# A fused attention and mixing kernel: wide key copies from one key buffer, and a newly searched order of all operations

## Chip, cores and metric

The kernel runs on one core of a Trainium2 chip. The metric is the time of one execution in microseconds (us) on the device. Several runs give a median, and one more execution was recorded by the hardware profiler. The core has TensorE (PE, matmuls), VectorE (DVE), ScalarE (ACT), GpSimd (POOL), and SyncE (SP), which here only issues transfers (DMA) between the device's memory and the on-chip memory.

## What is computed

Four batches of 768 positions, eight heads of 64, model width 512. Attention is over a local window and over 24 block summaries; what follows is a complex gate, a mixing over positions and a channel layer.

```python
def _attn_ref(q, k, v):                    # B, H, S, D = 4, 8, 768, 64
    block, window = (32, 16)
    k_sum = k.reshape(B, H, nb, block, D).max(axis=3)
    v_sum = v.reshape(B, H, nb, block, D).mean(axis=3)
    scores_l = scale * np.matmul(q, k.transpose(0, 1, 3, 2))
    mask_l = np.abs(pos[:, None] - pos[None, :]) < window
    scores_s = scale * np.einsum('bhsd,bhnd->bhsn', q, k_sum) + np.log(block)
    scores_all = np.concatenate([np.where(mask_l, scores_l, -1e9), scores_s], axis=-1)
    a = softmax(scores_all)
    return np.matmul(a, np.concatenate([v, v_sum], axis=2))
...
    theta = x @ w_theta
    zr, zi = x * np.cos(theta), x * np.sin(theta)
    y = np.einsum('ts,bsd->btd', w_tok_r, zr) + np.einsum('ts,bsd->btd', w_tok_i, zi)
    u = x + y
    return u + np.maximum(u @ w_ch, 0.0)
```

## The kernel before

**Tiles.** A tile is 128 positions of one batch, so there are 6 per batch and 24 in all; "tile n" counts through all batches. Heads are kept in four pairs, one pair filling the 128 partitions. For each tile the kernel does, on PE unless named otherwise:

- scores (L464): queries against a buffer `k` that holds, for each pair and each half of the tile, the 24 summaries and 94 neighbouring keys. `k` is filled by copies on ACT or POOL (L457): once a batch one copy of the summaries `ks` (192 elements a partition), and for each tile four copies of 2 pairs x 94 = 188 elements, one for each half of the tile and half of the pairs.
- softmax: DVE multiplies by the mask and takes sums (L502), ACT takes the exponential (L506);
- turns (L515, L519): transposes on PE, copied out by ACT or DVE;
- products with the values (L489) against two buffers `v`. Each half's values come by a DMA into one of four buffers; 24 rows of it hold the value summaries `vs`, which are copied there for the first tiles of a batch (L438). Norming is at L527 to L536;
- the second turn (L545), after which ACT copies out `x` (L296), or splits it into a high and a low part;
- theta (L570 for the first six tiles, as raw float32; L575 after that, split into parts);
- the gate: POOL or DVE reduces the angle (L587), DVE (L588) and ACT (L584, L593, L599) make sine and cosine, and DVE multiplies (L610), giving `zh`, and `zl` as the low part;
- a mixing step (L638) for each tile, half of the channels and pair of matrices, added into PSUM banks `m0`, `m1`, `m2`. At the end of a batch DVE adds the banks to `x` (L657).

**Keys and summaries.** At the start of a batch (`prepass`, L378 to L419) the keys come by DMA into two buffers `kn` of two pairs each; DVE takes the maxima of blocks (L387) and the sums of values `vt` (L409; for the first batch PE does it, L393).

**Weights.** These come as 64-bit floats and are turned into float32 by integer operations: a magnitude (L348 on ACT, L350 on DVE), a clamp (L352, POOL or DVE), a shift and two combinations on DVE (L354, L356, L359). This runs for all matrices in the first 85 us. High and low parts are made at L296/L298 and L305.

**The out stage** works on the last `u` with a Strassen-like scheme: operands are prepared (L679, L305), 56 products run on PE (L754), and DVE and ACT add them (L761, L766, L773).

**What sets the order.** All operations of the kernel (about 2000) are recorded once, and `schedule` (L226) replays them in the order of a table of numbers, `ORDER` (from L55), in which each number is a record and a letter behind it picks ACT (a), DVE (d) or POOL (g). Each engine takes its operations in the order in which the table has them, and SP issues the transfers likewise, waiting until the buffer of each is free. So a transfer whose buffer is still read holds up all transfers behind it.

Of the kernel before, what the change touches and what calls it, by code (L numbers as in the profile page):

```python
# [19 lines left out]
P = 128  # L20
NT = S // P
# [34 lines left out]
6 8 7 9 10 12 11 13 27g 22 29a 28a 31a 30a 32 1 33 41 42 46 34 14 0 161g 162g 66 16 4 44 45 37 35 67d 43 47 38 48 39 36 68d  # L56
40 69 70 3 71 18 15 17 19 163g 164a 60 2 51 691g 23 156 25 20 21g 49 24a 50a 165 61d 62g 63 64 26g 72 206 157 78 159 160g
158g 211g 209g 210g 212a 52d 166 5 167 168 169 53 174 176 177 175 213 170 171 73a 84 85 262 208 207 86 87 57a 54a 173 178
172 180 181 179 55 58 56d 59d 182 184 183a 185a 74g 75 65 193 79d 80g 186 214 217 216 81 76 82 222 215 77 83 266a 194a 220
187a 224 225 188 223 189d 268a 95a 267a 226 218 221 190a 191 96g 228 219 229 265a 227 97 192d 98 195 196 197 198 199 230 232  # L60
269 100a 200d 201 241 101g 231a 233a 270 272 273 322a 242a 202a 318 263 234 320 264 389 88 319 89 90 91 92 93 271 102 94 99
105 103 235a 236 278 280 281 274 106a 238a 239 323a 277 279 324g 107g 237d 240d 321a 275 284 276 285 282 283 108 104 109 243
244 245 246 247 248d 111d 286 288 325 287a 289a 203 249 112g 290 326 328 329 113 110 204 114 205 115 297 298a 299 254 300
250a 116a 251 291a 394a 121a 393a 255 301 256 302 253 334 336 327 292 335 332 333 338 339 293a 340 392a 330 331 303 117g
122d 252 118 123 119 124 120 125 304d 294a 126a 131a 337 295 305 310 342 311 257 296a 695a 341 353 344 395a 343a 345a 354a
306a 396 127g 132d 128 133 129 134 130 135 346 136a 141a 397 398 405 406 408 412 409 410 350a 307 355 356 357 358 137g 142d
138 143 139 144 140 308 145 347a 146a 359 151a 147d 360d 148 312 313 366 368 367 152g 348 361 351 349a 352a 693a 362a 424
425a 363 149 153 150 154 155 369 374 391 446 390 448 376 378 380 364 375 309 379 399 407 381 445 504 382 384 426 427 428 429
430 258a 689a 260a 431g 694g 696g 432 433a 434 400 377 401 411 402 450a 453a 404 454g 452g 451g 403 435 439 437 440 438 496
415 383 385 386 365 455 387 413 414d 416a 456 459 463 458 457 462 314g 315g 560 509a 692d 388g 449g 511g 460 510a 461 512a  # L70
259g 447g 498 417 497 464 467 465 418d 466 421a 422 513 468 470 469 471 505 507 508a 419 420d 423d 483 474 472 473d 484a
475a 514 517 516 261g 690d 506d 316d 485 486 476 487 488 564a 563a 370g 515 522 524 523 565a 518 566a 480a 525 557d 567 526
520 477a 527 519 521 489 529 528 481 478 479d 482d 530 532 531a 533a 490d 491 492d 493 697 499 698d 700d 699 534 568 570 436
494 574 541d 569 576 577 578 535a 536 538d 582 571 542d 573 575 572 605a 606a 537d 579 583 539 540d 701 702 543 545 703 317g
604g 580 595a 596d 495 584 704 581 586 705 706g 585d 707 546 551 636a 372a 544 770 587a 708a 607a 771a 637g 371g 601 608
654a 561 642a 547 553 549 562 588 589a 649 648 724 603 735 602 373g 609 653g 652g 441g 443a 444g 442g 500g 502g 501g 503g
773d 610 772 643g 613 611 612 614 617 619 621 592d 590 651a 593 618 591d 594d 620 616 622 615 623 624 597 774 598 775 625
599 776 627 777 709 778 626a 628d 555a 556d 779d 780 781a 638 600 639 640 644 655 629 799 641 645 646 685 647 686 687 802a
630a 656 633d 558g 559d 634 631 710 725 683d 664 800a 782 739g 659 663 738a 657 661 741a 666 684d 711 712d 801 713d 667 658
# [12 lines left out]
1068g 1009 996d 1034 1038 1003 1005 1182 1041 1183 1018 1134 1136 1019 1065 1064 1004 1043 1013 1184 1014 1185 1116a 1117
1058a 1042d 1007 1044d 1186 1187g 1118 1188 1189d 1015 1071 1045 1207 1016 1054 1056 1072 1046d 1190 1080 1081 1055 1057
1099a 1085 1148a 1075 1079 1146a 1191 1120a 1135 1049d 1053g 1059d 1100d 1121d 1208d 1050 1147g 1149g 1060 1062 1061 1063
1101 1103 1128 1143 1130 1228 1066 1138 1145 1144 1083 1119 1047 1048d 1073 1082 1074 1078 1087 1076 1086 1051d 1209 1077
1210a 1084 1211 1088 1212 1104 1213 1090 1214 1102 1150 1089a 1091a 1215 1092 1129 1137 1192 1216d 1217 1122d 1266 1126 1124
1127 1125 1151 1159 1161 1162 1218a 1267d 1093a 1153 1139 1268 1163 1193a 1160 1157 1096a 1166 1269a 1165 1152 1097 1094
1154 1095d 1155 1158 1156 1098a 1164 1270 1140 1271 1141 1169 1272 1167 1273 1142d 1006 1229 1131 1233a 1123g 1236g 1237g
1235a 1219 1230g 1197 1195 1198 1196 1194g 1220 1222d 1234a 1238 1308 1370 1231 1008 1168d 1170a 1274 1275g 1276 1171 1205
1201 1199 1172a 1316a 1223d 1239 1242 1241 1203 1277d 1287 1290a 1288a 1175a 1278 1309 1204 1010 1310g 1311 1247 1248 1289  # L100
1279 1250 1240 1173 1249 1176 1221 1174d 1177d 1315g 1243 1252 1251 1245 1246 1254 1314g 1232g 1253 1244 1313a 1224 1225
1291 1226 1292 1283 1293 1255 1294 1257 1227 1317 1256a 1295 1258a 1259 1280 1296d 1297 1345 1318 1319 1263a 1323 1264 1326
1320 1329 1321 1346d 1348a 1322 1298a 1333 1281d 1206 1421 1200 1372 1202 1371 1328 1260d 1261 1347 1373g 1374g 1330 1324
# [132 lines left out]
def c_dve(n, kind="psum"):  # L236

    return {"psum": 0.065 + n * 1.045e-3, "two": 0.05 + n * 1.045e-3, "fast": 0.045 + n * 0.52e-3}[kind]
# [30 lines left out]
def attn_moe(tc, qg, vg, kT, vT, vn, wth, wtr, wti, wch, cst, out, tune=TUNE):  # L269
# [154 lines left out]
    def att_tile(b, i, due):  # L424
# [19 lines left out]
        else:  # L444
# [512 lines left out]
```

## Time and profile before

| | us |
|---|---|
| median of 3 runs | 459.95 |
| the runs | 459.4, 459.95, 460.04 |
| the profiled execution | 458.47 |
| its span | 456.7 |
| granted TensorE clock | 1.00 |

The span is what the profiler's trace covers; the 1.8 us around it belong to the execution too. The profile's groups have one row for a line, engine, operation and tile: count, busy time and mean time in ns, then the idle time of the engine just before them with what ended it. A timeline row has the start, the length, the engine, the line and the operation, with its outputs and inputs, and in brackets the idle time before it and its releaser. In names, `k<-kn` reads: written `k`, read `kn`.

### The profile page before, as it was taken

The numbers are of one execution on the slowest core, as the hardware profiler recorded it, in microseconds if no ns is written. First come the engines' busy times: TensorE is split into PE (matmuls) and PEld (weight loads), VectorE is DVE, ScalarE is ACT, GpSimd is POOL, SyncE is SP. The second block draws the span as 40 slices with busy tenths as digits, with TensorE's granted clock in tenths as the row PEclk, the third lists the DMA queues.
The fourth block names the chain that finished last, engine by engine and source line by source line (L and its number), as shares of the span: only waits on it lengthen the run. The fifth ranks groups of instructions, "written<-read, shape, count | busy, mean of one in ns | idle before, by whom it ended". The sixth has DMA issues, their size and how long they took to land.

```text
span 456.7 us, 9383 instructions
## 1 busy us (share of the span) xinstructions
PE 436.5 (96%) x3552; PEld 355.6 (78%) x3552; DVE 336.3 (74%) x926; ACT 270.8 (59%) x608; POOL 103.0 (23%) x126
## 2 busy tenths in 40 slices
PE   1998999999999999999999999999999999999997
PEld 1465555667888788888888888888878878899996
DVE  3799899698296755776667644765455789999997
ACT  2699996888676677756376585676334316323420
POOL 0421103626910021211031102011111300163340
PEclk9999999999999999999999999999999999999999
DMA  8999965220458222310723400310004710000077
GB/s 286 336 329 282 414 201 155 89 60 4 132 177 275 83 71 72 105 54 12 252 79 105 132 4 1 117 37 1 0 1 140 253 70 0 1 0 1 18 267 269
DMA packets 25005, 55.80 MB, mean 122 GB/s; under 512 B 2944, under 2 KB 8320, under 8 KB 24960
## 3 DMA queue, kind: packets, MB, share of 16 engines
q1 hardware_dynamic: 24960, 55.20, 37.1%
q8 instruction: 28, 0.46, 0.4%
q14 instruction: 17, 0.14, 0.1%
HBM read 45.75 MB, written 9.44 MB: 121 GB/s over the span
## 4 chain that ended last, share of the span: by engine, by line
PE 58%; DVE 12%; issue 1%; ACT 0%; DVEq 0%
PE m L638 31%; PE t L575 9%; PE m L754 4%; PE c L754 4%; PE pa L489 3%; DVE wt L305 3%; PE s L464 3%; PE pa L515 2%; DVE cb L679 2%; PE t L545 2%; DVE x L657 1%; DVE cu L773 1%; PE t L754 1%; DVE zl L305 1%; DVE wth L305 1%
## 5 line engine op out<-in xcount | busy, mean ns | idle before, releaser
L638 PE MATMUL m<-wt,zh 128*128 128x512 f32 (+1 forms) x768 | 181.1, 359 | 2.8 <-DVE zh L610 1.5
L638 PEld LDWEIGHTS m<-wt,zh 128*128 128x128 f32 x768 | 122.5, 188 | 35.1 <-issue 14.3
L638 PE MATMUL m<-wt,zl 128*128 128x512 f32 x336 | 85.9, 336 | 0.0
L506 ACT ACTIVATE e<-e,st 128x118 f32<-128x118 f32 x192 | 64.0, 388 | 22.7 <-DVE st L502 21.9
L638 PEld LDWEIGHTS m<-wt,zl 128*128 128x128 f32 x336 | 51.2, 188 | 7.3
L502 DVE CUSTOM_DVE_ANT_0 e<-s,cs 128x118 f32<-128x118 f32 x192 | 45.3, 273 | 4.8 <-PE s L464 4.2
L575 PE MATMUL t<-wth,xh 128*128 128x512 f32 x144 | 48.0, 414 | 0.1
L464 PE MATMUL s<-k,q 64*64 64x118 f32 x768 | 25.9, 273 | 10.7 <-POOL k L457 10.6
L584 ACT ACTIVATE w<-t,bmagic 128x512 f32<-128x512 f32 x24 | 16.5, 686 | 32.2 <-PE t L575 21.4
L464 PEld LDWEIGHTS s<-k,q 64*64 64x64 f32 x768 | 20.4, 136 | 16.5 <-POOL k L457 10.7
L489 PEld LDWEIGHTS pa<-v,e 118*64 118x64 f32 x768 | 24.9, 137 | 6.5 <-issue 2.5
L489 PE MATMUL pa<-v,e 118*64 118x65 f32 x768 | 28.3, 224 | 1.4 <-DMA v<-vg 0.9
L515 PEld LDWEIGHTS pa<-cs,e 128*118 128x118 f32 x192 | 22.7, 136 | 8.9 <-ACT e L506 2.0
L515 PE MATMUL pa<-cs,e 128*118 128x128 f32 x192 | 29.2, 275 | 0.3
L575 PE MATMUL t<-wth,xl 128*128 128x512 f32 x72 | 28.4, 394 | 0.0
L610 DVE TENSOR_TENSOR w<-xn,w 128x512 f32<-128x512 f32 x18 | 12.3, 686 | 20.0 <-ACT w L600 19.9
L457 POOL COPY k<-kn 128x188 f32<-128x188 f32 x40 | 13.0, 347 | 59.9 <-DVE st L529 17.0
L588 DVE CUSTOM_DVE_ANT_0 w<-t,w 128x512 f32<-128x512 f32 x24 | 16.5, 688 | 13.2 <-POOL w L587 12.8
L657 DVE TENSOR_TENSOR x<-m,x 128x512 f32<-128x512 f32 (+1 forms) x32 | 16.3, 549 | 12.7 <-PE m L638 12.7
L575 PEld LDWEIGHTS t<-wth,xh 128*128 128x128 f32 x144 | 22.0, 189 | 2.6 <-DVE xl L551 0.4
L305 POOL TENSOR_TENSOR zl<-zb,zh 128x512 fp32r<-128x512 f32 x9 | 11.8, 1309 | 51.9 <-DVE vs L418 16.5
L587 DVE TENSOR_SCALAR w<-w 128x512 f32<-128x512 f32 x17 | 7.2, 424 | 21.5 <-ACT w L584 21.5
(169 smaller groups left out, 802.0 us busy)
## 6 DMA issues: line engine op xcount, KB each, us to landing
v<-vg SPq DMA_DIRECT2D x48, 195.0 KB, 4.1
q<-qg SPq DMA_DIRECT2D x24, 256.0 KB, 4.1
kn<-kT SPq DMA_DIRECT2D x6, 798.0 KB, 6.3
wt<-wtr SPq DMA_DIRECT2D x6, 768.0 KB, 11.0
wt<-wti SPq DMA_DIRECT2D x6, 768.0 KB, 12.2
f<-vT SPq DMA_DIRECT2D x12, 384.0 KB, 3.3
cu<-u_scratch SPq DMA_DIRECT2D x8, 384.0 KB, 6.8
out<-x SPq DMA_DIRECT2D x16, 192.0 KB, 2.2
```

Source lines behind the costliest of these rows:

```text
L305: lambda e: V[e].tensor_tensor(dst(), src(), hi().bitcast(F32), op=ALU.subtract), reads, writes, due, port=BOTH)
L464: scores = (0.79 if len(parts) == 1 else 2.1, [lambda p=p, g=g, h=h, c=c, kk=kk: nc.tensor.matmul(sc[h].get()[ROW[g], p, c], q.get()[ROW[h ...
L489: mm(2 * 0.433 + scores[0] + (0.2 if scores[0] else 0.0), [lambda n=n, g=g, a=a: nc.tensor.matmul(xa[a].get()[ROW[g], n], turned[a].get()[ ...
L502: op({"DVE": 0.205}, lambda eng, n=n: nc.vector.tensor_tensor_reduce(e()[:, n], sc[n % 2].get()[:, 2 * a + n // 2], mask(m), -SCALE, 3.0e3 ...
L506: op({"ACT": 0.288}, lambda eng, n=n: nc.scalar.activation(e()[:, n], e()[:, n], AF.Exp, bias=st.get()[:, n:n + 1], scale=-1.0), [(st, n)] ...
L515: mm(NH * 0.109, [lambda n=n: nc.tensor.transpose(tp.get()[:NK, n], e()[:, n], ident()) for n in range(NH)], [e_ref, (cs, "ident")], [tp], ...
L575: calls = [lambda t=t, xx=xx, k=k, c=c: nc.tensor.matmul(th.get(), xx.get()[:, c], w_th[c].get()[:, k], start=(c == 0 and t == 0), stop=(c ...
L584: op({"ACT": 0.59}, lambda e: nc.scalar.activation(r(), th.get(), AF.Identity, bias=bmagic.get(), scale=1.0 / TWO_PI), [th, bmagic], [R], due)
L588: op({"DVE": c_dve(DM)}, lambda e: nc.vector._custom_dve(TENSOR_ADD_SAT, out=r(), in0=th.get(), in1=r(), s0=PI_F, s1=-PI_F), [th], [R], due)
L638: nc.tensor.matmul(acc[th](), zz.get()[:, r, cc], w[:, TT[th]], start=(s == 0 and r == 0 and t == 0 and (th == 0 or c == 0)), stop=(s == N ...
L657: op({"DVE": c_dve(nt * P)}, lambda e, u=u, acc=acc: nc.vector.tensor_tensor(u(), acc(), u(), op=ALU.add), [areg] + [(xs, n) for n in rang ...
L754: calls = [lambda k=k, t=t, x=x, y=y: nc.tensor.matmul(to.get(), weights[n][x][0]()[:, k, j * P:(j + 1) * P], operands[n].get()[:, y, k], ...
```

## The change

It has two parts.

**Keys.** `prepass` allots one buffer `kn` of four pairs in place of two of two. A tile then needs two key copies of 4 pairs x 94 = 376 elements in place of four of 188. The branches that fed scores straight from `kn` (`DIRECT`) and that ran a tile's scores within the products' operation are gone; `KB`, `WARM` and `SP0` are new settings whose values (1, 0, 0) give one `k` buffer a batch, no idle code ahead, and unsplit scores.

**Order.** `ORDER` is a new table for the renumbered operations. Constants of the planner (`c_dve`, the magnitude's cost) differ, too, but only the table decides the order. Among the assignments that changed: key copies go from 56 on ACT and 40 on POOL to 23 and 25; the summaries' copies of the value buffers from 6 on ACT, 1 on DVE and 9 on POOL to 4, 4 and 8; low parts of the mixing matrices and of the out stage's operands from 19 on POOL to 12, the others to DVE; three magnitudes of the early weights from DVE to ACT.

```diff
     def prepass(b, due):
-        kn = [Ref(apool, [P, 2, S + 2 * HALO], tag="kn", bufs=K["KN"]) for _ in range(2)]
+        kn = Ref(apool, [P, NP, S + 2 * HALO], tag="kn")
         step = 1 if b == 0 else 2
         for p in range(0, NP, step):
-            t, here = kn[p // 2], slice(p % 2, p % 2 + step)
+            here = slice(p, p + step)
...
-            copies, whole = [], kbuf[b] is None
-            if whole:
-                kbuf[b] = Ref(apool, [P, NP, 2, NK], tag="k")
-            k = kbuf[b]
-            if whole:
-                copies += [(lambda: k.get()[..., :NB], lambda: ks.get()[:, :, None].broadcast_to((P, NP, 2, NB)), 2 * NP * NB, [ks], "sum")]
-            for a in range(2):
-                for g in range(2):
-                    copies += [(lambda a=a, g=g: k.get()[:, 2 * a:2 * a + 2, g, NB:],
-                                lambda a=a, g=g: kn[a].get()[:, :, (2 * i + g) * QT:(2 * i + g) * QT + NL], 2 * NL, [kn[a]], (a, g))]
+        k = Ref(apool, [P, NP, 2, NK], tag="k", bufs=K["KB"]) if i < K["KB"] else kbuf[b][i % K["KB"]]
+        def copy(dst, src, n, rd, wr):
+            op({"POOL": c_pool(n, False), "ACT": c_act(n)},
+               lambda e: (nc.scalar.copy if e == "ACT" else V[e].tensor_copy)(dst(), src()), rd, wr, due, port=BOTH)
+        parts = [range(0, 2), range(2, 4)] if b * NT + i < K["SP0"] else [range(NP)]
+        for r in parts:
+            pp = slice(r.start, r.stop)
+            if i < K["KB"]:
+                copy(lambda pp=pp: k.get()[:, pp, :, :NB], lambda pp=pp, n=len(r): ks.get()[:, pp, None].broadcast_to((P, n, 2, NB)), 2 * len(r) * NB,
+                     [(ks, x) for x in r], [(k, (x, "sum")) for x in r])
+            for g in range(2):
+                copy(lambda g=g, pp=pp: k.get()[:, pp, g, NB:], lambda g=g, pp=pp: kn.get()[:, pp, (2 * i + g) * QT:(2 * i + g) * QT + NL],
+                     len(r) * NL, [(kn, x) for x in r], [(k, (x, g)) for x in r])
...
-TUNE = dict(... VB=4, KN=2, DIRECT=0, FUSE=99, ...)
+TUNE = dict(... VB=4, KB=1, WARM=0, SP0=0, FUSE=99, ...)
...
 ORDER = """
-6 8 7 9 10 12 11 13 27g 22 29a 28a 31a 30a 32 1 33 41 42 46 34 14 0 161g 162g 66 16 4 44 45 37 35 67d 43 47 38 48 39 36 68d
+6 12 7 13 10 11 8 9 27a 28g 22 29g 30 0 14 1 31 39 42 33 3 64 32 34 40 65d 66d 5 41 35 37 38 43 46 44 45 16 18 15 17 19 58
```

Lines move by two or three; after the change the scores stay at L464, key copies are at L447, value copies at L442, DMA at L287, products at L487, second turns at L543, raw theta at L568, and mixing steps at L636.

**Three places in the new order.** A number behind a name is the record of its buffer; x2 stands for two like rows in a row.

POOL at the start of the program, from the first key copies to those of tile 2. Before (`k_86` is the key buffer, `v_218` and the like are value buffers, `xh` a part of a weight matrix):

```order
L457 COPY k_86<-ks_78 128x8x24
L457 COPY k_86<-kn_75 128x2x94 x2
L457 COPY k_86<-kn_81 128x2x94
L298 CAST wth1_171<-xl_138 128x512
L418 MEMSET vs_179 24x8
L352 ISA
L352 TENSOR_SCALAR xh_208<-xh_208 128x512
L438 COPY v_177<-vs_179 24x520
L438 COPY v_222<-vs_179 24x520
L438 COPY v_218<-vs_179 24x520
L457 COPY k_86<-kn_81 128x2x94
L457 COPY k_86<-kn_75 128x2x94 x2
```

Now:

```order
L447 COPY k_85<-kn_75 128x4x94 x2
L422 MEMSET vs_157 24x8
L447 COPY k_85<-kn_75 128x4x94 x2
L442 COPY v_171<-vs_157 24x520
L447 COPY k_85<-kn_75 128x4x94
L442 COPY v_215<-vs_157 24x520
L442 COPY v_219<-vs_157 24x520
```

POOL has the two wide copies of tile 0 and of tile 1, and one of tile 2 (the other is on ACT), and the copy for tile 2 stands ahead of two of the three value copies; before, all three were ahead of tile 2's.

SP's transfers for tile 3 and the next ones, each in the order of issue. Before (`v_218` and `v_222` take tile 3's values, `v_177` here takes tile 4's first half; `q` are queries):

```order
L290 DMA q_454<-qg 128x512
L290 DMA v_218<-vg 96x520
L290 DMA v_177<-vg 96x520
L290 DMA v_222<-vg 96x520
L290 DMA q_477<-qg 128x512
```

Now, with `v_219` and `v_215` for tile 3 and `wt` for mixing matrices:

```order
L287 DMA q_472<-qg 128x512
L287 DMA v_219<-vg 96x520
L287 DMA wt_494<-wtr 128x1536
L287 DMA wt_496<-wti 128x1536
L287 DMA v_215<-vg 96x520
L287 DMA q_499<-qg 128x512
```

Tile 4's load no longer stands between the two of tile 3; two weight loads do.

PE from the products of tile 3 on, around the turns of tile 2 (`t<-cs,xn`) and its first theta product (`t<-xh,x`). Before:

```order
L489 MATMUL pa1_586<-v_222,e_571 64x65
L545 MATMUL t_609<-cs_112,xn_518 128x128 x4
L570 MATMUL t_615<-xh_208,x_369 128x512
L638 MATMUL m0_617<-wt_496,zh_603 128x512
L638 MATMUL m2_619<-wt_496,zh_603 128x256
L570 MATMUL t_615<-xl_138,x_369 128x512
```

Now:

```order
L487 MATMUL pa1_571<-v_219,e_555 64x65
L636 MATMUL m0_615<-wt_517,zh_584 128x512
L636 MATMUL m2_617<-wt_517,zh_584 128x256
L543 MATMUL t_619<-cs_113,xn_525 128x128 x4
L636 MATMUL m0_615<-wt_517,zh_584 128x512
L636 MATMUL m2_617<-wt_517,zh_584 128x256
L568 MATMUL t_627<-xh_154,x_319 128x512
L568 MATMUL t_627<-xl_130,x_319 128x512
```

Mixing matmuls of the first step have moved around the turns, so two of them now stand between the turns and the first theta product that reads their result.

More of the change, by code (lines that the diff above doesn't have):

```diff
@@ L236, in c_dve @@
 def c_dve(n, kind="psum"):
-    return {"psum": 0.065 + n * 1.045e-3, "two": 0.05 + n * 1.045e-3, "fast": 0.045 + n * 0.52e-3}[kind]
+    return {"psum": 0.063 + n * 1.045e-3, "two": 0.065 + n * 1.045e-3, "fast": 0.07 + n * 0.52e-3}[kind]
 def c_act(n, psum=False):
@@ L327, in attn_moe @@
     op({"DVE": 0.1}, lambda e: nc.vector.memset(beps.get(), 1e-9), [], [beps], -100.0)
+    if K["WARM"]:
+        pr.key = ("WARM", 0)
+        idle, bank = Ref(tpool, [P, DM], tag="zb", bufs=K["ZS"]), Ref(pt, [P, DM], tag="t", bufs=K["PS_T"])
+        op({"DVE": 0.31, "POOL": 0.3}, lambda e: V[e].memset(idle.get(), 0.0), [], [idle], -100.0, port=BOTH)
+        for _ in range(K["WARM"]):
+            mm(c_raw(DM), [lambda: nc.tensor.matmul(bank.get(), idle.get()[:, :P], idle.get(), start=True, stop=True)], [idle], [bank], -100.0)
+        pr.key = ("", 0)
     def load_f64(j, tag, src, n, due, token=(), pool=wpool, bufs=1):
@@ L350, in magnitude @@
                 nc.vector.tensor_scalar(f().bitcast(I32), hi(), 0x7fffffff, None, ALU.bitwise_and)
-        op({"ACT": c_act(n), "DVE": c_dve(n, "fast")}, magnitude, [raw], [f_ref], due, port=BOTH)
+        op({"ACT": c_act(n) + n * 1.05e-4, "DVE": c_dve(n, "two")}, magnitude, [raw], [f_ref], due, port=BOTH)
         op({"POOL": c_pool(n, False), "DVE": c_dve(n, "fast")}, lambda e: V[e].tensor_scalar(
@@ L460, in att_tile @@
+        if i < K["KB"]:
+            kbuf[b].append(k)
         m = 0 if i == 0 else (2 if i == NT - 1 else 1)
@@ L463, in att_tile, with scores @@
         sc = [Ref(ps, [P, NP, NK], tag=f"s{h}") for h in range(2)]
-        scores = (0.79 if len(parts) == 1 else 2.1, [lambda p=p, g=g, h=h, c=c, kk=kk: nc.tensor.matmul(
-            sc[h].get()[ROW[g], p, c], q.get()[ROW[h], p, ROW[g]], kk(p, g, ROW[h]), start=True, stop=True)
-            for p in range(NP) for c, kk in parts for g in range(2) for h in range(2)], [q] + reads, sc)
-        if b * NT + i >= K["FUSE"]:
-            products(scores)
-        else:
-            products()
-            pr.late, pr.key = K["R_SM"], ("S", b * NT + i)
-            mm(*scores, due, mode="score")
+        def scores(pairs):
+            mm(0.79 * len(pairs) / NP, [lambda p=p, g=g, h=h: nc.tensor.matmul(
+                sc[h].get()[ROW[g], p], q.get()[ROW[h], p, ROW[g]], k.get()[ROW[h], p, g], start=True, stop=True)
+                for p in pairs for g in range(2) for h in range(2)], [q] + [(k, (x, y)) for x in pairs for y in ("sum", 0, 1)], [(x, y) for x in sc for y in pairs], due, mode="score")
+        products()
+        pr.late, pr.key = K["R_SM"], ("S", b * NT + i)
+        for pairs in parts:
+            scores(pairs)
         xn[b, i] = Ref(apool, [P, H, D], tag="xn", bufs=K["XNB"])
```

177 lines of the change are left out of this document (82 added, 95 removed).

## The prediction

> **What bounds the kernel now.** I read the page's busy times and its chain first, then the windows by stage, then the waits of PE, and last the timeline at each wait.
>
> ```profile
> PE 436.5 (96%) x3552; PEld 355.6 (78%) x3552; DVE 336.3 (74%) x926; ACT 270.8 (59%) x608; POOL 103.0 (23%) x126
> PE 58%; DVE 12%; issue 1%; ACT 0%; DVEq 0%
> ```
>
> TensorE (PE) is busy for 96% of the span, and the chain runs through it for most of its length. The change leaves PE's 3552 matmuls as they are, in number and shape. So a gain can only come out of time in which PE waits, and a loss only from new waits. The windows by stage (start to end, length, then busy time of PE, of its weight loads, DVE, ACT and POOL, the granted clock, the DMA share and GB/s) say which engine stands close behind PE:
>
> ```profile
> 10.00:24.00 14.00, 13.27 (x153) 7.15 (x153) 9.89 (x50) 8.07 (x24) 5.35 (x13) 1.00 1.05 338
> 24.00:85.60 61.60, 57.73 (x425) 34.16 (x425) 58.08 (x149) 54.52 (x125) 13.13 (x18) 1.00 0.78 256
> 85.60:366.00 280.40, 279.11 (x2491) 232.82 (x2489) 180.02 (x594) 176.32 (x407) 61.95 (x78) 1.00 0.29 92
> 366.00:437.00 71.00, 69.99 (x395) 65.45 (x394) 68.86 (x105) 26.02 (x42) 19.02 (x11) 1.00 0.04 14
> ```
>
> From 24 to 85.6 us, where the weights are converted, DVE is as busy (58.08 of 61.60 us) as PE (57.73), and ACT is busy for 54.52: there DVE sets the pace. From 85.6 to 366 us PE is alone at the limit. In the out stage DVE (68.86 of 71.00) is close behind it again. The clock is 1.00 throughout.
>
> ```profile
> PE s L464 <- POOL k L457: 10.6, 2, 10.0
> PE m L638 <- DVE zh L610: 1.5, 2, 1.0
> PE m L638 <- DVE x L657: 1.2, 4, 0.5
> PE pa L489 <- DMA v<-vg: 0.9, 1, 0.9
> PE t L570 <- ACT x L296: 0.7, 1, 0.7
> PE pa L489 <- PE t L575: 0.5, 1, 0.5
> PE c L754 <- DVE w L305: 0.3, 1, 0.3
> ```
>
> These are the waits of PE (total, times, longest). They come to 15.7 us here, and 10.0 of that is the start. So about 5.7 us lie inside the kernel, and this is all that an order can give.
>
> **The start doesn't move.**
>
> ```profile
> 10.03 1.85 PE L464 MATMUL s<-k,q 64*64 64x118 f32 x32 [10.03 <-POOL k L457]
> 7.56 2.01 DVE L387 TENSOR_REDUCE ks<-kn 128x24 f32<-128x768 f32 x2 [1.78 <-DMA kn<-kT]
> 9.63 0.34 POOL L457 COPY k<-ks 128x192 f32<-128x192 f32 x1 [9.18 <-DVE ks L387]
> 8.67 0.60 ACT L457 COPY k<-kn 128x188 f32<-128x188 f32 x2 [1.91 <-DMA kn<-kT]
> ```
>
> The first scores wait for the last part of the keys (ACT's copies start at 8.67, just behind its landing), for the last two maxima on DVE (to 9.57) and for the copy of the sums (9.63 to 9.97). All three remain. After the change the two wide key copies are on POOL and the copy of the sums on ACT: the wide copies can run from about 8.65 to 9.65, beside the last maximum. I count 0 for the start; if a wide copy took 0.65 us in place of 0.50, it would be 0.3 worse.
>
> **The wide copies.** Of before, 96 copies of 188 elements move keys (56 on ACT, 40 on POOL), after it 48 of 376 (23 and 25).
>
> ```profile
> L457 POOL COPY k<-kn 128x188 f32<-128x188 f32 x40 | 13.0, 347 | 59.9 <-DVE st L529 17.0 <-DVE zh L298 11.4 <-PE pa L515 8.7
> L457 ACT COPY k<-kn 128x188 f32<-128x188 f32 x56 | 18.7, 345 | 3.3 <-DMA kn<-kT 1.9 <-PE s L464 1.4
> L438 POOL COPY v<-vs 24x520 f32<-24x520 f32 x9 | 5.4, 609 | 7.3 <-DVE w L595 5.4 <-DVE xh L356 1.3 <-ACT vs L416 0.5
> L296 ACT COPY x<-t 128x512 f32<-128x512 f32 x16 | 9.5, 592 | 7.8 <-PE t L545 4.3 <-DVE xl L551 2.1 <-DVE xh L298 1.3
> ```
>
> No row shows 376 elements. POOL takes 347 ns for 188 and 609 for 520, ACT 345 for 188 and 592 for 512. The line between them gives 347 + 262 x 188/332 = 495 ns on POOL and 345 + 247 x 188/324 = 488 on ACT (the bounds are one narrow copy, 347, and two, 694). Copying then takes 25 x 0.495 + 23 x 0.488 = 23.6 us in place of 31.7, so 8 us less on ACT and POOL over the whole kernel. Neither is the bound, so this is worth nothing by itself; what counts is the few places where PE waits for a copy. Against it stand four more activation table loads on ACT, all behind the first stage, where ACT is idle for over 100 us:
>
> ```profile
> L599 ACT ACT_TABLE_LOAD x13 | 16.7, 1283 | 0.2
> L348 ACT ACTIVATE f<-wt 128x768 f32<-128x768 f32 x11 | 10.1, 934 | 1.5 <-DMA wt<-wtr 1.0 <-DVE wt L359 0.5
> ```
>
> Each is 1.28 us, 5.1 together. (The second row, one magnitude of the weights on ACT, is used below.)
>
> **The places where PE waits in the first 85 us.**
>
> ```profile
> 19.73 1.73 POOL L438 COPY v<-vs 24x520 f32<-24x520 f32 x3 [1.35 <-DVE xh L356]
> 21.42 0.91 POOL L457 COPY k<-kn 128x188 f32<-128x188 f32 x3
> 22.14 1.26 PE L464 MATMUL s<-k,q 64*64 64x118 f32 x32 [0.60 <-POOL k L457]
> 27.25 8.98 SPq L290 DMA_DIRECT2D v<-vg  x3
> 41.42 1.15 PE L489 MATMUL pa<-v,e 118*64 118x65 f32 x30 [0.94 <-DMA v<-vg]
> 43.82 1.12 PE L570 MATMUL t<-xh,x 128*128 128x512 f32 x2 [0.67 <-ACT x L296]
> 81.55 1.56 PE L638 MATMUL m<-wt,zh 128*128 128x512 f32 x4 [1.02 <-DVE zh L610]
> ```
>
> At 22.14 tile 2's scores wait for POOL, which had three value copies (1.73 us) ahead of the key copies; after, one wide copy stands on POOL with only one value copy ahead and the other on ACT. I expect these 0.60 to go.
>
> At 41.42 tile 3's products wait for its second value load. SP had been held for about 9 us ahead of it, by tile 4's load into a buffer that tile 2 still read. After, both loads of tile 3 stand ahead of tile 4's. As many weight and query loads stand ahead as before, and one value load (195 KB) less. At the 256 GB/s of this stage that is 0.76 us earlier, so I expect 0.7 to 0.94 of the wait to go.
>
> At 43.82 the first theta product waits for ACT's copy of x. After, half of a mixing step (two matmuls) stands behind the transposes and half ahead of them, so the copy has cover: 0.67 goes.
>
> But these 2.2 us aren't all kept, for DVE sets the pace until 85 us, and the wait at 81.55 shows it: 1.02 us for DVE's zh of tile 4. After, tile 6's scores and turns (some 2.3 us of PE) stand ahead of this step, and DVE has two more reductions ahead of it, as the row below prices them, with the rest about even: 1.7 to 1.9 us more.
>
> ```profile
> L409 DVE TENSOR_REDUCE vt<-f 128x24 f32<-128x768 f32 x12 | 11.2, 948 | 0.0
> DVE zb L610 <- ACT w L600: 1.0, 1, 1.0
> ```
>
> With DVE's own idle time unchanged, the step starts 1.7 later while 2.3 us of PE's work have moved ahead of it: a net gain of 0.6. On top comes what DVE itself no longer loses. It waits 1.0 us for ACT's sine (second row, tile 2), behind the theta products whose wait at 43.82 goes; I take 0.6 of it. **Early gain: 1.2**, between 0 (DVE finds new waits of its own) and 3.7 (the four waits go and the later ones don't take their place).
>
> **The middle and the out stage.**
>
> ```profile
> 152.94 0.73 PE L638 MATMUL m<-wt,zh 128*128 128x256 f32 x3 [0.17 <-DVE x L657]
> 294.33 0.74 PE L638 MATMUL m<-wt,zh 128*128 128x256 f32 x3 [0.48 <-DVE x L657]
> 337.20 1.15 PE L489 MATMUL pa<-v,e 118*64 118x65 f32 x32 [0.47 <-PE t L575]
> 397.77 2.18 PE L754 MATMUL c<-wt,w 128*128 128x384 f32 x11 [0.27 <-DVE w L305]
> ```
>
> At 152.94 three quarters of a theta product now stand between, and at 337.20 matmuls of tile 22's theta have moved between turn and products: 0.17 + 0.47 = 0.64 goes. At 294.33 and twice near 367 PE's order is the same, and so are those waits. In the out stage DVE's work ahead of the product at 397.77 shrinks by some 9 us, as operand preparations moved behind it; its 0.27 goes, and two smaller delays like it at 407 and 418, 0.2 together. Against that a mixing step near 204 us has less PE work between it and the one that frees its bank: up to 0.3 lost, of which I count 0.1. **Sum: 0.64 + 0.27 + 0.2 - 0.1 = 1.0**, between 0 and 1.5. The last product and the end of the span are the same in both.
>
> **Total.** 1.2 + 1.0 = 2.2 us off the profiled execution's 458.47 gives 456.3. The runs' median, 459.95, lies 1.48 above the profiled execution, so the forecast is **457.8 us**. If everything shown went, it would be 3.7 + 1.5 = 5.2 less, 454.8.
>
> [...]
>
> ```profile
> L305 DVE TENSOR_TENSOR wt<-cb,wt 128x768 fp32r<-128x768 f32 x10 | 10.8, 1100 | 0.0
> L305 DVE TENSOR_TENSOR wt<-cu,wt 128x768 fp32r<-128x768 f32 x4 | 3.8, 948 | 0.0
> ```
>
> The same subtraction takes 948 ns in one group and 1100 in the other, so something stretches DVE's instructions by up to 150 ns on the mean. [...]
>
> **The rivals.**
>
> *DVE keeps the pace, and nothing is left to measure.* A POOL copy of 0.50 in place of 0.35 us may hold up the DVE instruction beside it by 0.15 us more. Six or seven of them stand ahead of the step at 81.55: 1.0 us, which leaves 0.2 of the early gain. With a new wait of 0.3 near 204 and half of the out stage's gain, the total is 0.2 + 0.64 + 0.25 - 0.3 = 0.8: **459.2**. For it speaks that DVE is busy for 94% of the stage (58.08 of 61.60); against it, that fewer POOL copies are issued, and that the sum of POOL's copying falls.
>
> *Slower: DVE waits for ACT in the first 85 us.* In the stage where both are almost full, three magnitudes move from DVE to ACT, and wide copies stand in ACT's order ahead of the softmax and of the magnitudes that DVE needs next. One magnitude is about 0.93 us on ACT and a wide copy 0.49. If DVE waits for two such pairs, 2 x 1.4 = 2.8 us, the step at 81.55 starts 2.8 later, against the 1.2 gained; with the middle's new wait as in the first rival, and its out gain, it is 1.6 - 0.6 = 1.0 longer: **461.0**. It decides once DVE's waits between 24 and 85.6 us grow by over about 2.2 us (they are 61.60 - 58.08 = 3.5 now). For it: ACT is busy for 54.52 of 61.60. Against it: ACT's work ahead of the mixing steps of tiles 3 and 4 falls by over 2 us, by counts and durations of groups.
>
> *The order doesn't do what it says.* If the wide copies took two narrow ones' time, 694 ns, ACT and POOL would win nothing, and the gaps between the scores of two tiles (1.0 to 1.5 us of PE) would just hold two copies, 1.4. The order's own gains stay: 0.4 to 0.8 lost, **458.4**. This lies inside the forecast's own range.
>
> **How the numbers follow.** I give the forecast, with the third rival in it, 0.64 (its own range is 454.8 to 459.0), the first rival 0.19, the slower one 0.17. A measurement of this kernel can tell about 0.2%, 0.9 us, from no change. So faster holds the forecast and a small part of the first rival, less the forecast's upper end: 0.63; within 0.2%, 0.20; slower, 0.17. The range goes from 454.6 to 461.0: it takes in nearly all that the waits could give and reaches to the slower case.
>
> **What would show it.** In the changed kernel's waits of PE the rows for the copies of keys should have 10.0 us once and nothing at tile 2, and the row for the value load should be gone or below 0.25. The wait for ACT's x should be gone. At the first mixing step of tile 4 PE should still wait for DVE. Wide copies of 0.48 to 0.52 us would bear out the line through the two sizes; 0.65 or more speaks for the third rival. More DVE idle time than 3.5 us between 24 and 85.6 us, with ACT as the releaser, is the slower rival. What would make the forecast wrong above all is a new PE wait in the middle, where hardly any is now and where the order has moved most.

## The result and the profile after

The changed kernel takes 464.63 us (median of 6 runs, 461.96 to 465.46) where the kernel before, beside it, takes 458.75 (457.11 to 460.04): a ratio of 1.0115, with a 95% interval of 1.0082 to 1.0149. It is slower by about 1%. A later comparison gave 463.82 and 1.0094 (1.0060 to 1.0128). One execution of the kernel with four places mended, below, was in a slow state (726.41 us at a granted clock of 0.564) and is in none of the medians and ratios. The profiled execution's span is 462.2 us, 5.5 more than before.

The page's line of busy times and the windows by stage, in the columns of before:

```profile
PE 438.3 (95%) x3552; PEld 356.0 (77%) x3552; DVE 335.0 (72%) x918; ACT 277.2 (60%) x588; POOL 97.9 (21%) x107
```

```profile
10.00:24.00 14.00, 12.31 (x120) 5.66 (x121) 9.13 (x49) 7.47 (x20) 3.73 (x9) 1.00 1.05 318
24.00:85.60 61.60, 57.98 (x458) 34.39 (x459) 59.57 (x152) 55.48 (x117) 14.66 (x23) 1.00 0.77 260
85.60:366.00 280.40, 275.84 (x2455) 228.92 (x2454) 178.31 (x581) 180.52 (x400) 54.32 (x56) 0.99 0.26 83
366.00:437.00 71.00, 70.35 (x403) 65.75 (x402) 64.44 (x101) 26.16 (x43) 16.87 (x12) 1.00 0.16 57
```

The loss is in the third row. PE had been busy for 279.11 of these 280.40 us, and is now for 275.84, with 36 matmuls fewer; and the granted clock of the stretch reads 0.99, so some of that busy time is slow besides. The waits of PE show what it waits for:

```profile
PE s L464 <- ACT k L447: 10.6, 1, 10.6
PE m L636 <- DVE x L655: 2.8, 3, 1.8
PE pa L513 <- ACT e L504: 1.8, 3, 0.7
PE s L464 <- POOL k L447: 1.5, 2, 1.0
PE s L464 <- DVE st L527: 1.0, 1, 1.0
PE pa L513 <- ACT vs L420: 0.8, 1, 0.8
PE pa L513 <- ACT xn L532: 0.7, 1, 0.7
PE t L543 <- DVE w L586: 0.6, 1, 0.6
PE pa L487 <- ACT e L517: 0.3, 1, 0.3
PE pa L513 <- DVE xn L534: 0.2, 1, 0.2
```

All rows sum to 20.3 us, against 16.2 for all of before's (the seven rows in the prediction are 15.7 of it): 4.1 more. With the slow clock below (1.6 us) that is 5.7, near the 5.5 of the spans. So the losses of this execution are new waits, and a clock that falls behind some of them. That the sums agree so closely is in part chance: the last stage has become 1.2 us shorter (see the out stage below), which these rows hardly show.

**The place near 266 us.** PE's timeline, first three rows, and then ACT's and DVE's:

```profile
266.76 0.32 PE L513 MATMUL pa<-cs,e 128*118 128x128 f32 x1 [0.73 <-ACT e L504]
267.61 0.32 PE L513 MATMUL pa<-cs,e 128*118 128x128 f32 x1 [0.53 <-ACT e L504]
268.46 0.48 PE L513 MATMUL pa<-cs,e 128*118 128x128 f32 x2 [0.53 <-ACT e L504]
...
264.08 0.93 ACT L532 ACTIVATE xn<-pa,st 128x64 f32<-128x64 f32 x4 [4.23 <-DVE zb L608]
265.01 1.28 ACT L504 ACT_TABLE_LOAD   x1
266.31 2.10 ACT L504 ACTIVATE e<-e,st 128x118 f32<-128x118 f32 x7
...
263.37 0.67 DVE L608 TENSOR_TENSOR zb<-xn,w 128x512 f32<-128x512 f32 x1
```

PE waits three times for ACT's exponentials of tile 19, 1.79 us in all. ACT is not busy ahead of them: it stands for 4.23 us at the second norm of tile 18 (`xn`, L532). That norm's own inputs were ready at 259.1; but there are three `xn` buffers, so tile 18's is tile 15's, and DVE reads that one last at 263.37 to 264.04 (`zb<-xn`, L608). Eight exponentials and the load of their activation table wait behind the norm. In the kernel before, the norm stands behind the exponentials:

```profile
263.24 0.68 ACT L506 ACTIVATE e<-e,st 128x118 f32<-128x118 f32 x2
263.82 0.88 ACT L534 ACTIVATE xn<-pa,st 128x64 f32<-128x64 f32 x4
```

The windows of the changed kernel just behind the waits, with the clock as the third column from the end:

```profile
268.00:270.00 2.00, 1.54 (x5) 1.16 (x6) 0.69 (x1) 1.21 (x4) 0.00 (x0) 0.68 0.00 0
270.00:272.00 2.00, 2.00 (x8) 1.78 (x7) 0.00 (x0) 0.89 (x2) 0.00 (x0) 0.50 0.00 0
```

At 0.68 and 0.50 for 2 us each, PE loses 0.64 + 1.00 = 1.6 us more, an estimate from the clock; PE's busy time is 1.8 us longer than before's (438.3 against 436.5) for the same matmuls.

**The place near 338 us.** PE's row, and ACT's and DVE's ahead of it:

```profile
338.44 0.74 PE L636 MATMUL m<-wt,zh 128*128 128x256 f32 x3 [1.77 <-DVE x L655]
...
327.53 1.28 ACT L597 ACT_TABLE_LOAD   x1
330.09 1.28 ACT L504 ACT_TABLE_LOAD   x1
332.82 0.68 ACT L582 ACTIVATE w<-t,bmagic 128x512 f32<-128x512 f32 x1
...
336.05 0.69 DVE L295 CAST xh<-t 128x512 fp32r<-128x512 f32 x1 [1.37 <-ACT x L293]
336.77 0.69 DVE L549 TENSOR_TENSOR xl<-t,xh 128x512 fp32r<-128x512 f32 x1
337.38 1.01 DVE L655 TENSOR_TENSOR x<-m,x 128x512 f32<-128x512 f32 x2
```

The mixing step needs its bank emptied by DVE's addition (L655). Its input is complete about 336.4, but DVE has two operations in front of it that split tile 22's `x` into its high and low part (`xh`, `xl`), and those come late, since ACT's reduction (L582), behind two table loads and five exponentials, had held up the chain that frees their bank.

Smaller new waits are at 124.57 us (0.52, a key copy), 204.63 (0.41, an addition), 81.45 (0.96, key copies) and 84.52 (0.80, the value summaries).

### The profile page after: what moved, and what is told of

It is laid out like the page before. It is cut to its first block, busy times and chain, and to the rows that moved or that the text cites. A ratio compares the mean times of both kernels' runs of the same rounds, so it can differ in the third digit from the quotient of the medians.

```text
span 462.2 us, 9342 instructions
## 1 busy us (share of the span) xinstructions
PE 438.3 (95%) x3552; PEld 356.0 (77%) x3552; DVE 335.0 (72%) x918; ACT 277.2 (60%) x588; POOL 97.9 (21%) x107
## 4 chain that ended last, share of the span: by engine, by line
PE 77%; DVE 13%; ACT 5%; issue 2%; DMA 2%; POOL 1%; SPq 0%; POOLq 0%; DVEq 0%
PE m L636 36%; PE t L573 10%; PE c L752 6%; PE m L752 5%; PE s L464 5%; PE pa L487 4%; PE pa L513 4%; PE t L543 2%; DVE wt L363 2%; DVE f L360 2%; PE pa L397 2%; DMA kn<-kT 2%; DVE e L500 1%; ACT e L504 1%; PE t L752 1%
## 5 line engine op out<-in xcount | busy, mean ns | idle before, releaser
L636 PE MATMUL m<-wt,zh 128*128 128x512 f32 (+1 forms) x768 | 181.5, 359 | 2.8 <-DVE x L655 2.8
L636 PEld LDWEIGHTS m<-wt,zh 128*128 128x128 f32 x768 | 122.8, 189 | 34.9 <-issue 14.1
L636 PE MATMUL m<-wt,zl 128*128 128x512 f32 x336 | 86.5, 338 | 0.0
L636 PEld LDWEIGHTS m<-wt,zl 128*128 128x128 f32 x336 | 51.2, 188 | 7.3
L500 DVE CUSTOM_DVE_ANT_0 e<-s,cs 128x118 f32<-128x118 f32 x192 | 44.3, 272 | 7.1 <-PE s L464 4.9
L573 PE MATMUL t<-wth,xh 128*128 128x512 f32 x144 | 49.1, 423 | 0.0
L464 PE MATMUL s<-k,q 64*64 64x118 f32 x768 | 25.9, 273 | 13.2 <-ACT k L447 10.6
L464 PEld LDWEIGHTS s<-k,q 64*64 64x64 f32 x768 | 20.4, 136 | 19.7 <-POOL k L447 12.7
L513 PE MATMUL pa<-cs,e 128*118 128x128 f32 x192 | 30.0, 279 | 3.6 <-ACT e L504 1.8
L513 PEld LDWEIGHTS pa<-cs,e 128*118 128x118 f32 x192 | 22.8, 138 | 13.0 <-ACT e L504 4.7
L582 ACT ACTIVATE w<-t,bmagic 128x512 f32<-128x512 f32 x24 | 16.6, 691 | 22.5 <-PE t L573 19.1
L487 PEld LDWEIGHTS pa<-v,e 118*64 118x64 f32 x768 | 24.5, 137 | 6.6 <-issue 3.8
L447 POOL COPY k<-kn 128x376 f32<-128x376 f32 x25 | 13.4, 548 | 75.6 <-DMA kn<-kT 22.2
L517 ACT COPY e<-pa 118x512 f32<-118x512 f32 x34 | 19.2, 587 | 16.7 <-PE pa L513 16.6
L487 PE MATMUL pa<-v,e 118*64 118x65 f32 x768 | 27.8, 224 | 0.3 <-ACT e L517 0.3
L517 DVE COPY e<-pa 118x512 f32<-118x512 f32 x14 | 9.6, 688 | 21.2 <-PE pa L513 21.2
L302 POOL TENSOR_TENSOR zl<-zb,zh 128x512 fp32r<-128x512 f32 x13 | 16.9, 1305 | 34.9 <-DVE zh L295 13.7
L293 ACT CAST wt<-cb 128x768 fp32r<-128x768 f32 x13 | 10.7, 837 | 19.4 <-POOL cb L677 11.8
```

The costliest lines, as they stand in the source:

```text
L302: lambda e: V[e].tensor_tensor(dst(), src(), hi().bitcast(F32), op=ALU.subtract), reads, writes, due, port=BOTH)
L464: mm(0.79 * len(pairs) / NP, [lambda p=p, g=g, h=h: nc.tensor.matmul(sc[h].get()[ROW[g], p], q.get()[ROW[h], p, ROW[g]], k.get()[ROW[h], p ...
L487: mm(2 * 0.433 + scores[0] + (0.2 if scores[0] else 0.0), [lambda n=n, g=g, a=a: nc.tensor.matmul(xa[a].get()[ROW[g], n], turned[a].get()[ ...
L500: op({"DVE": 0.205}, lambda eng, n=n: nc.vector.tensor_tensor_reduce(e()[:, n], sc[n % 2].get()[:, 2 * a + n // 2], mask(m), -SCALE, 3.0e3 ...
L513: mm(NH * 0.109, [lambda n=n: nc.tensor.transpose(tp.get()[:NK, n], e()[:, n], ident()) for n in range(NH)], [e_ref, (cs, "ident")], [tp], ...
L517: lambda e: (nc.scalar.copy if e == "ACT" else nc.vector.tensor_copy)(t.get()[:NK], tp.get()[:NK].rearrange("k n q -> k (n q)")), [tp], [t ...
```

## The experiments

Each ratio is to the kernel before, run beside it. The edits move operations within `ORDER` (shown by the numbers around them) unless said otherwise.

### The changed kernel again

> The changed kernel unchanged, for a second profile. Theory (places): the losses stand at fixed places of the order, so the second profile has the same waits of PE within 0.3 us each: three for ACT's exponentials near 266 us (0.5 to 0.7 each), one for the additions near 338 (1.8), key copies near 81 and 124. Rival (clock): the losses go with the granted clock of 0.996; then a run at 1.000 lacks most of them and is 2 us or more shorter. Rival (landing): the first scores' start at 10.56 in place of 10.03 is a matter of when the keys land, and varies by some 0.5 us from profile to profile.

Measured: 463.82 us, ratio 1.0094 (1.0060 to 1.0128). The waits near 266 and 338 us are there again, to the tenth:

```profile
PE s L464 <- ACT k L447: 9.9, 1, 9.9
PE m L636 <- DVE x L655: 2.8, 3, 1.8
PE pa L513 <- ACT e L504: 1.8, 3, 0.7
```

The first scores start at 9.9 us in place of 10.56, so the start varies from execution to execution, and the clock theory falls in its simple form: in this kernel's ten runs, the five with a clock of 0.996 have medians of 464.2 and 464.1 us in the two comparisons, the five at 1.000 medians of 465.1 and 463.6. In these ten runs a fall of the clock shows no price that can be told.

### The norm behind the exponentials

```diff
-1223 1224d 1263 1227a 1290 1284 1282
+1292 1243a 1285 1227a 1333g 1334g 1309
```

> The changed kernel with one operation moved: ACT's second norm of tile 18 behind eight exponentials of tile 19. Theory (places): ACT stood 4.2 us at this norm, whose buffer was still read by DVE, with ready exponentials behind it. Moved, PE's three waits near 266 us (1.8 together) go, and the time falls by 1.8 us if the waits are all, by about 4.3 if the slow matmuls behind them (the clock there reads below 1) come from the waits. Rival (width of copies): the time stays within 0.5 us, since the loss comes from elsewhere.

Measured: 461.71 us, ratio 1.0048 (1.0028 to 1.0068), 2.1 less than the changed kernel. The row of waits for exponentials at the turns (L513 <- ACT e) is gone from the trace, and the profiled span is 457.7. One token moved takes back nearly half of the loss. The gain of medians is 2.1 and not 4.3. A part of that is the clock: 7 of its 12 runs still have 0.996 or less, and are 0.8 us longer in the median than the other five. Where the clock fell in them no trace shows, for the profiled one is at 1.000. The rest of the difference stays open.

### The late reader moved instead

```diff
-1272d 1274d 1288 1241 1281 1289 1280
...
-1280 1262 1242 1223
+1273 1331 1257 1241 1242 1258d 1259
```

> The changed kernel with the late reader moved in place of the waiting norm: DVE's two multiplications of tile 15's gate (their operands are ready at 251 us, and they ran at 261.6 and 263.4) stand ahead of the reduction of tile 16's angle, where DVE idles. Theory (places, with the buffer as the cause): the norm of tile 18 finds its buffer free, PE's three waits near 266 us go with ACT's order untouched, and the time falls as in e1, by about 2 us to 461.7. Rival (the norm's place by itself, or the table load behind it): the waits near 266 us stay above 1 us in sum, and the time stays near 463.8.

Measured: 461.79 us, ratio 1.0051 (1.0028 to 1.0073), the same as with the norm moved. ACT's order is as in the changed kernel, but its norm no longer waits:

```profile
251.61 0.67 DVE L608 TENSOR_TENSOR w<-xn,w 128x512 f32<-128x512 f32 x1
252.21 0.67 DVE L608 TENSOR_TENSOR zb<-xn,w 128x512 f32<-128x512 f32 x1
...
259.20 0.95 ACT L532 ACTIVATE xn<-pa,st 128x64 f32<-128x64 f32 x4
260.18 1.28 ACT L504 ACT_TABLE_LOAD   x1
261.47 2.11 ACT L504 ACTIVATE e<-e,st 128x118 f32<-128x118 f32 x7
```

The table load of 1.28 us is there as before, and the row of PE's waits for exponentials at the turns (L513 <- ACT e) is gone. So the cause of the waits near 266 us is the buffer: a reader late on DVE, and the writer's place at the head of ACT's queue.

### The place near 338 us alone

```diff
-1507 1534d 1535d 1573 1574d 1575 1586 1589a 1587d 1588 1537 1540 1541 1538
+1456a 1496 1556 1573 1506 1504 1501
...
+1537 1540 1541 1587d 1588 1538 1559a
```

> The changed kernel with the place near 338 us mended alone (DVE's conversions of tile 22 behind the two additions, ACT's reduction of tile 21's angle ahead of five exponentials). Theory (places): PE's wait of 1.8 us for an addition falls to 0.8 or less, and the time by about 1.2 us, to 462.6; the waits near 266 us stay. Rival (slack): what is gained at 338 us is lost again at the next wait for an addition near 374 us, and the time stays at 463.8 within 0.4.

Measured: 462.69 us, ratio 1.0072 (1.0043 to 1.0101). By the ratios that is 1.0 us less than the changed kernel, but the two intervals overlap. The trace tells more: the waits for additions fall from 2.8 to 1.8 us, the longest from 1.8 to 0.8, and the one near 374 us, where the rival has the gain lost again, stays at about 0.6 (1.8 less the 0.8 and the 0.41 near 204 us, an estimate). So this wait is not lost again there; what it is worth in time this run alone can't tell.

### The two long waits together, and the two small ones alone

The first kernel has the edits of the norm and of 338 us; the second has only these:

```diff
-608a 687 487g 631g 618 582 619
+488a 608a 687 631g 487g 618 582
...
-1008 1145a 975 973 979 1082a 1020a
+963a 1008 1145a 973 975 979 1082a
```

> The changed kernel with only the two long waits mended, near 266 us (the norm) and near 338 us. Theory (long waits cost twice, by themselves and by the clock that falls behind them): with both gone the granted clock is 0.999 or more in nearly all runs, and the ratio to the kernel before is 1.000 to 1.002, that is 3 us or more less than the changed kernel, more than the 2.1 of e1 and the 1.2 of e7 would leave if each kept a fallen clock. Rival (only the waits count): ratio 1.0026 or more, by 1.0094 less 0.0046 less 0.0022, and runs with the clock near 0.996 stay as common as in e1 (7 of 12).

Measured: 459.58 us, ratio 1.0015 (0.9996 to 1.0033). All 12 runs have a clock of 0.998 or more. The interval takes in the rival's 1.0026 too, so the times alone don't part the two; the clocks do, for the rival has about 7 such runs of 12. Against the kernel with the norm alone the ratio is lower by 0.0033, or 1.5 us, which is at the edge of the noise.

> The changed kernel with only the two small places of e5 mended: tile 10's key copy ahead of the subtraction on POOL (near 123 us), and the 512-wide addition ahead of the 256-wide one (near 204 us). Theory (places, each worth its own wait): 0.5 + 0.4 = 0.9 us less than the changed kernel, ratio 1.0075 in place of 1.0094; the long waits near 266 and 338 us and the clock below 1 behind them stay. Rival (slack): these small gains are lost at the next wait, ratio 1.009 or more.

Measured: 462.1 us, ratio 1.0083 (1.0051 to 1.0115), between the two expectations and with an interval over both. By itself this settles nothing. Its profile, at a clock of 1.000, has both long waits (1.8 us each) with no fall behind either; its other five runs have 0.995 or 0.996.

### All four places

The edits of the norm, of 338 us and the two small ones together:

> The changed kernel with four places mended, without the maxima of e4: the norm of e1; near 338 us DVE's conversions of tile 22 behind the two additions, and ACT's reduction of tile 21's angle ahead of five exponentials; tile 10's key copy ahead of a subtraction on POOL; and near 204 us the 512-wide addition of batch 1 ahead of the 256-wide one. Theory (places): e4 without its loss near 80 us, and 0.4 for the addition: 1.5 to 2 us less than e1, so about 460.0, level with the kernel before within 0.2%. Rival: e4's gain behind 94 us was chance, and the time stays at e1's 461.7.

Measured: 458.62 us (median of 11 runs), ratio 0.9994 (0.9968 to 1.0020). The same kernel again, with its profile:

> The kernel of e5 once more, for a profile of an undisturbed execution. Theory (places): in its trace the waits near 266 us and the one for key copies near 124 are gone, the one for an addition near 204 is below 0.2, the one near 338 at most 0.9, and the granted clock is 1.000; the span is 456 to 457.5, as before's. Rival: its time came from elsewhere, and some of these waits are still there.

Measured: 457.81 us, ratio 0.9987 (0.9969 to 1.0004). The span is 456.0 us, the clock 1.000. Its five longest rows of waits of PE:

```profile
PE s L464 <- ACT k L447: 10.6, 1, 10.6
PE m L636 <- DVE x L655: 1.4, 2, 0.8
PE s L464 <- ACT e L504: 1.1, 1, 1.1
PE pa L513 <- ACT xn L532: 1.0, 2, 0.7
PE s L464 <- POOL k L447: 0.9, 1, 0.9
```

The waits near 124, 204 and 266 us are gone, and the one near 338 is 0.8. So these four places hold the loss of the changed kernel, as far as can be measured: with them mended it is level with the kernel before.

### A mend that went wrong, and two more places

A kernel with three of these four places (without the addition near 204 us) had the maxima of batch 1's keys moved ahead of a sum on DVE, too, to shorten the wait at 81.45:

```diff
-365 369 667d 371 418 419g 420 367 396 388
+365 369 667d 367 371 418 419g 420 396 388
```

> The changed kernel with five places mended: the norm as in e1; DVE's conversions of tile 22 behind the two additions of batch 2's end, and ACT's reduction of tile 21's angle ahead of five exponentials (near 338 us); the maxima of batch 1's second half ahead of a sum (near 79 us); and tile 10's key copy ahead of a subtraction on POOL (near 123 us). Theory (places): 4.3 + 1.0 + 0.5 + 0.5 = 6.3 us less than the changed kernel, about 458, level with before. Rival (width): 462 or more, as the mended places don't carry the loss.

Measured: 462.2 us, ratio 1.0051 (1.0025 to 1.0077), though it held three of the four edits that give 458.6. The trace shows why, in PE's timeline and in the windows:

```profile
83.12 0.47 PE L513 MATMUL pa<-cs,e 128*118 128x128 f32 x1 [1.74 <-ACT e L504]
```

```profile
83.00:86.00 3.00, 2.20 (x9) 1.51 (x10) 0.35 (x2) 2.21 (x6) 2.34 (x4) 0.50 0.00 0
86.00:88.00 2.00, 2.00 (x5) 0.97 (x4) 1.49 (x9) 0.40 (x1) 2.00 (x4) 0.50 0.00 0
```

The maxima (1.74 us on DVE) now stand ahead of tile 4's angle, so ACT waits 3.29 us for it in place of 1.70, and the exponentials of tile 5, behind the sine and a table load, are late: a new wait of 1.74, and a clock of 0.50 from 82.7 to 89.5 us. By the ratios, what I expected as a gain of 0.5 cost 2 to 3 us.

The last kernel added two gentler edits there to the four places (DVE's conversion 667 behind 378; PE's steps 482 and 483 up, around 401):

> The kernel of e5 with two more places mended between 77 and 88 us: DVE's conversion of a theta matrix moves from ahead of the maxima of batch 1 to a stretch where DVE idles, and on PE the first two mixing steps of tile 4 move up, one ahead of tile 5's last turn and one behind it. Theory (places): scores of tile 6 wait 0.4 us less, the wait of 0.8 for the value summaries goes: 0.9 less than e5, so 457.8 against 458.7, faster than the kernel before by 0.2%. Rival: DVE sets the pace there, and the time is e5's within 0.4 us.

Measured: 458.05 us, ratio 0.9986 (0.9969 to 1.0002), the same as its neighbour without them (457.81 in the same comparison). The wait for the value summaries is gone from the trace, and others of 0.2 to 0.5 us came in its place: there the rival was right. No version here is clearly faster than the kernel before.

### The wide copies alone

The kernel before with its own order; one `kn` buffer, and two copies of 376 elements a tile, each at the place of the later of the two that it replaces:

```diff
-for a in range(2):
-    for g in range(2):
-        copies += [(lambda a=a, g=g: k.get()[:, 2 * a:2 * a + 2, g, NB:], ..., 2 * NL, [kn[a]], (a, g))]
+for g in range(2):
+    copies += [(lambda g=g: k.get()[:, :, g, NB:], ..., 4 * NL, [kn], g)]
```

> The kernel before, with its own order, and one change: one key buffer and two wide copies a tile, each at the place of the later of the two narrow ones that it replaces. Theory (places): the same time as before, within 1 us (459 +- 1), as PE hardly waits for copies. Rival (width): wide copies hold up POOL, ACT and DVE, and the kernel is slower by 2 us or more, with new waits of the scores for copies.

Measured: 460.24 us, ratio 1.0015 (0.9993 to 1.0036): no difference that can be told, and at most 0.36%, or 1.7 us. So the copies' width by itself is at most about a third of the loss, and maybe none of it; the order is the main cause. Narrow copies in the new order were not run.

## Why the prediction was wrong

I forecast 457.8 us, with 461.0 as the upper end; it is 464.6. The step that failed is the middle's, below.

- **What bounds it:** right. PE's work is the same (the same 3552 matmuls), and the loss found is time in which PE waits or runs at a lower clock.
- **The start, 0:** borne out as far as it can be seen. It was 10.56 us in one profile and 9.9 in the next of the same kernel, and from 9.7 to 10.6 in all profiles of the new order, so the 0.5 of the first is no effect of the change.
- **The wide copies:** their size was about right on ACT and a tenth too small on POOL; alone they are worth nothing that can be measured. First the groups of the copies in the changed kernel, then POOL's and DVE's timeline near 123 us:

```profile
L447 POOL COPY k<-kn 128x376 f32<-128x376 f32 x25 | 13.4, 548 | 75.6 <-DMA kn<-kT 22.2 <-DVE zb L608 15.8 <-DVE w L593 13.4
L447 ACT COPY k<-kn 128x376 f32<-128x376 f32 x23 | 11.5, 499 | 1.0 <-PE s L464 1.0
```

```profile
121.49 1.85 POOL L302 TENSOR_TENSOR wt<-wt 128x768 fp32r<-128x768 f32 x1 [8.14 <-DVE zl L302]
123.29 1.22 POOL L447 COPY k<-kn 128x376 f32<-128x376 f32 x1
122.46 1.69 DVE L302 TENSOR_TENSOR wt<-wt 128x768 fp32r<-128x768 f32 x1
```

  548 and 499 ns, against 495 and 488. One of POOL's took 1.22 us while DVE's subtraction beside it took 1.69, where the same subtraction at 117.36 us, with POOL idle, takes 0.95: both are long here, where they overlap. The group of 1100 ns in the prediction shows the same: two of its ten subtractions ran beside POOL's work and took 1.88 and 1.54 us, the other eight, with POOL idle, 0.94 to 0.95. From the timeline of the kernel before:

```profile
419.79 1.85 POOL L679 TENSOR_TENSOR cb<-x,cb 128x768 f32<-128x768 f32 x1 [0.49 <-DVE cu L773]
420.57 1.88 DVE L305 TENSOR_TENSOR wt<-cb,wt 128x768 fp32r<-128x768 f32 x1
433.56 1.02 POOL L298 CAST wt<-x 128x768 fp32r<-128x768 f32 x1 [2.81 <-DVE cu L773]
433.86 1.54 DVE L305 TENSOR_TENSOR wt<-cb,wt 128x768 fp32r<-128x768 f32 x1
```

  That each of six or seven wide copies holds DVE up by 0.15 us more, as the first rival has it, was my estimate from 0.50 less 0.35; no run shows such a term, and what was measured is the one place near 123 us. PE waited 0.52 us for that copy. At the group's mean of 0.55 it would have ended by 123.84, before PE was ready at 124.05 (an estimate from these rows); and with the copy ahead of POOL's subtraction the wait is gone as well. So the price is paid at one place, not on the average of 25, and the order and the overlap both have a part in it.
- **The early gain, 1.2:** not there, at the low end of its bounds. PE's busy time from 10 to 85.6 us is 70.29 us, 0.7 less than before, with the first execution's late start (0.5) in it. The waits that I said would go did mostly go (the value load's 0.94 is no more in the list, the one for ACT's x neither), but waits of 1.04 (23.95 us, tile 2's scores, now for DVE), 0.57 (44.85), 0.65 (52.62), 0.96 and 0.80 took their place. PE's wait for DVE's `zh`, which the sum let stay at tile 4's mixing step, is gone too.
- **The middle, 0.64 less 0.1:** here is the step that failed. The waits at 152.94 and 337.20 went as forecast. But I took the middle's losses from one place only (204 us, where 0.41 came), counted 0.1 for it, and bounded them by what PE has between neighbouring steps of its own. I did not follow the queues of ACT and DVE where "the order has moved most", nor the reuse of the `xn` buffers. The prediction's last sentence names such a wait as what would make it wrong above all, and gives it no price. The four places of the experiments are all of this kind: 0.52 + 0.41 + 1.79 + 1.77 = 4.5 us of waits, and in the profiled execution 1.6 of clock, where the sum had a gain of 0.54. That the loss is theirs is shown by the kernels that mend them, 458.62 and 457.81 us.
- **The out stage, 0.47:** the wait at 397.77 is gone from the list, as forecast, and the single wait of 0.62 near 375 us is about the two of 0.29 before. But the gain is over twice the forecast. The last 479 matmuls, before and after, from the last wait for an addition to the end of the span:

```profile
368.14:456.70 88.56, 84.80 (x479) 80.58 (x479) 83.03 (x128) 28.76 (x47) 22.01 (x13) 1.00 0.20 72
374.80:462.20 87.40, 84.03 (x479) 80.12 (x479) 78.74 (x127) 29.61 (x48) 20.71 (x13) 1.00 0.20 73
```

  That is 1.16 us less, and ahead of this point the changed kernel loses 6.7 us, not 5.5. PE's busy time for these matmuls fell by 0.77, so "all that an order can give" was not bounded by the list of waits, as I had it.
- **The slower rival** had the right kind of mechanism (an engine that stands at one operation, with ready work behind it), at the wrong place and with the engines exchanged: it was ACT that waited for DVE, in the middle, where both are idle for a third of the time (DVE is busy for 178.31 and ACT for 180.52 of 280.40 us). I had priced it only where the engines are full, and there it didn't come: DVE's idle time from 24 to 85.6 us fell from 3.5 to 2.0 us. The price of the place near 266 us was 2.1 us; with the two long waits mended, the rest of the loss (0.15%) can no longer be told from none.

## What to carry to other kernels

When a new order is to be priced, the busy share of an engine doesn't bound what it can cost (ACT, busy for 180.52 of the middle's 280.40 us, stood for 4.23 at one norm with eight exponentials behind it, and PE then waited 1.79 for them): go through each in-order queue and ask of every instruction when its output buffer comes free, by counting buffers and finding the last reader of the one it takes, and what stands behind it. Long waits can be dearer than their length: in the kernels with one of about 1.8 us a clock of 0.996 or less came in 39 of 62 runs, in those with none above 1.3 us inside in 6 of 153. And where a search has set an order, mending the two or three longest waits by hand, one to three tokens each, tells quickly whether the order or the change itself is at fault.

## What the runs showed of the hardware

In the five profiles with a fall of the granted clock, it came at waits of 1.74 to 1.79 us (one wait, or three within 2.5 us): 0.2 us behind the last one's end in the two profiles of the changed kernel, 0.4 us ahead of it in the kernel with the maxima moved, and in the other two within the same stretch of 5 us as the wait (the clocks of these stretches are 0.94 and 0.93). It lasted 3.4 us at 0.50 in four of them and 6.8 us in the kernel with the maxima moved, as the clocks of the windows work out. A mean of 0.996 is what one such fall makes of a whole span (1 - 1.7/462), so the mean tells of each run whether there was one, but not where. In the kernel with the late reader moved, the fall is behind the wait at 338 us:

```profile
330.00:335.00 5.00, 3.14 (x17) 2.45 (x16) 2.46 (x5) 1.10 (x2) 0.00 (x0) 0.94 0.00 0
335.00:340.00 5.00, 5.00 (x24) 4.26 (x23) 1.33 (x3) 0.59 (x1) 0.00 (x0) 0.72 0.02 3
```

In the changed kernel and in the one with the norm moved, the same wait (1.77 and 1.8 us) is followed by a full clock. So such a wait makes a fall likely and not certain: 7 of 12 runs of the norm's kernel, 6 of 12 with the reader moved and 6 of 10 with only 338 us mended have a clock of 0.996 or less, and those runs are 0.8, 1.4 and 1.7 us longer in the median (in the changed kernel, with 5 of 10, no such difference is seen). With both long waits mended, and none above 1.2 us left inside the kernel, it is 0 of 12. Nor is a shorter wait quite safe: the kernel before, with 1.0 as its longest, has 5 of 96 in the four later comparisons, and the one with four places mended 1 of 21; where the clock fell in those runs no trace shows.
